# An adaLN attention block on one core: the first scale blocks move to ScalarE's queue, and the order of the k stage is redone

## The chip, the core and the metric

The kernel runs on one NeuronCore of a Trainium2 chip. The metric is the device time of one execution in microseconds (us). Thirteen runs of the kernel before gave a median of 98.5 us, from 97.48 to 99.33 us.

## What is computed

The reference is an attention layer with adaptive layer normalisation. With B = 2, N = 256, D = 1152 and all inputs in bf16:

```python
mod = (silu(c) @ w_mod).reshape(B, 6, 1, D)
shift_a, scale_a, gate_a = mod[:, 0], mod[:, 1], mod[:, 2]
h = layernorm(x) * (1 + scale_a) + shift_a
q, k, v = split(h @ wqkv)
p = softmax(q @ k.T * D ** -0.5)
return x + gate_a * (p @ v) @ wo
```

Three of the six parts of `w_mod` are used: shift, scale and gate. The host packs them, and the four other weights, so that each load is a block of whole rows for the 128 partitions.

## The kernel before

The 512 rows of x are four tiles of 128 tokens (t = 0 to 3; tiles 0 and 1 are batch 0, tiles 2 and 3 batch 1). D is nine slices of 128 (k = 0 to 8). The kernel first computes K transposed, one contraction slice k after the other, so that it can begin when the first rows of wK are there. This "k stage" is what the change touches. After it come Q (`wQ`), the scores, V (`wV`), the softmax, P·V and the output projection, all unchanged.

The parts of the k stage, by the names of their helpers:

- **Statistics.** Tiles 0 and 2 take their mean and variance on VectorE: three `stat_chunk` (bn_stats over 384 columns), then `stat_aggr`, then `stat_ln` and `stat_exp` on ScalarE give 1/std. Tiles 1 and 3 take them on ScalarE: `stat_sum` and `stat_sq` (two passes over 1152 columns), `stat_ln2`, `stat_exp`.
- **Normalise and transpose.** `norm(t, k0, k1)` on VectorE writes xn; `transposes(t, h)` on TensorE puts slices 0-1 (h = 0) or 2-8 (h = 1) into one of two PSUM buffers of the pool `psum_tp`; `evac_tp` copies them to xnT on ScalarE or VectorE.
- **Scale.** `silu_c` makes silu(c) and GpSimd repeats it into `scT_rep`. `scale_mods(gi, 0, 9)` multiplies it with one group of `wS` columns into the PSUM tile `psS` (which already holds ones); `copy_s1p(gi)` copies 1 + scale to SBUF. The groups are slices 0-1, 2-3, 4-5 and 6-8. `scaled_tp` takes the product straight from the transposes' PSUM tile; `scaled` (both tiles of a batch) and `scaled_t` (one tile) take it from xnT. All write hTs.
- **The products.** `k_step(k, n0, n1)` makes nine matmuls (one for each slice f of the output) over tokens n0 to n1 of batch 0. `k_step_b1(k, fs)` does the same for batch 1 and the listed f. Only f = 0 to 4 of batch 1 are accumulated in this pass; f = 5 to 8 follow later from the finished hTs.

The order is written out by hand. Each engine's instructions are recorded (`_Rec`, line 70, so that almost every instruction carries line 70 in the profile), and `pin` fixes that order (line 668). The long list of helper calls from line 307 to line 429 is therefore the order of TensorE, VectorE, ScalarE and SyncE at once: a call that stands earlier there stands earlier on its own engine.

Loads: x tiles, wK rows, scale groups and everything later go through SyncE's (SP) queue in the order of the list; only c goes through ScalarE's (ACT) queue (line 106). The order on SP is x0, x1, x2, scale group 0, wK0, x3, scale group 1, wK1, wK2, wK3, scale group 2, scale group 3, wK4 to wK8, then the shift, Q, gate, V and output weights. The framework gives each load one of eight completion semaphores in the order of its emission, and starts again with the first after the eighth. A load that takes a semaphore again waits on its issuing engine until the load that had it before has landed.

TensorE begins with dummy matmuls of ones (`junk(2)`, then the transpose of c and a matmul that fills psS with ones, then `junk(9)`), and only then comes to the transposes of x tile 0.

Of the kernel before, what the change touches and what calls it, by code (L numbers as in the profile page):

```python
# [15 lines left out]
def kernel(  # L16
# [14 lines left out]
    P = 128  # L31
    B, N, D = x.shape
# [68 lines left out]
    def load_x(eng, t):  # L101
        eng.dma_start(out=x_sb[:, t, :], in_=x_f[t * P : (t + 1) * P, :])

    nc.scalar.preload_act_table_set("natural_log_exp_and_others")
    load_x(syn, 0)
    sca.dma_start(out=c_sb, in_=c.rearrange("b (k p) -> (b k) p", p=P))

    wmpool = ctx.enter_context(tc.tile_pool(name="wmpool", bufs=1))
    wK = wpool.tile([P, KT, D], BF16)
# [11 lines left out]
        return rows  # L121

    wS_all = wmpool.tile([P, KT * D], BF16, tag="wS")
    S_GROUPS = SCALE_GROUPS
    wS = []
    for gi, (k0, k1) in enumerate(S_GROUPS):
        wS.append(wS_all[:, KT * P * k0 : KT * P * k1].rearrange("p (kk n) -> p kk n", kk=KT))
# [1 line left out]
    def load_scale(gi):  # L129
        k0, k1 = S_GROUPS[gi]  # L130
        cols = slice(KT * P * k0, KT * P * k1)
        src = w_scale[P * cols.start : P * cols.stop].rearrange("(p n) -> p n", p=P)
        syn.dma_start(out=wS_all[:, cols], in_=src)

    def load_wK(k):
        load_rows(wK[:, k : k + 1, :], wk[k])
# [37 lines left out]
    def stat_chunk(t, ch):  # L174
        vec.bn_stats(out=stats_t[t][:, ch, :], in_=x_sb[:, t, ch * CW : (ch + 1) * CW])

    def stat_aggr(t):
        vec.bn_aggr(out=mv_all[:, t, :], in_=stats_t[t])

    def stat_ln(t):  # L180
        sca.activation(out=lnv[:, t : t + 1], in_=mv_all[:, t, 1:2], func=ACT.Ln, bias=eps_t)

    def stat_exp(t):
        sca.activation(out=rstd[:, t : t + 1], in_=lnv[:, t : t + 1], func=ACT.Exp, scale=-0.5)
# [6 lines left out]
    def stat_sum(t):  # L191
        act_stats.add(t)
        sca.activation(out=scr, in_=x_sb[:, t, :], func=ACT.Copy, scale=-1.0 / D, accum_out=nmean[:, t : t + 1])

    def stat_sq(t):
        sca.activation(out=scr, in_=x_sb[:, t, :], func=ACT.Square, bias=nmean[:, t : t + 1],
                       accum_out=ssq[:, t : t + 1])

    def stat_ln2(t):
        sca.activation(out=lnv[:, t : t + 1], in_=ssq[:, t : t + 1], func=ACT.Ln, scale=1.0 / D, bias=eps_t)  # L200

    def norm(t, k0, k1):
        cs = slice(k0 * P, k1 * P)
        m_ap, m_op = (nmean[:, t : t + 1], ALU.add) if t in act_stats else (mv_all[:, t, 0:1], ALU.subtract)
        vec.tensor_scalar(
            out=xn[:, t, cs], in0=x_sb[:, t, cs], scalar1=m_ap,
            scalar2=rstd[:, t : t + 1], op0=m_op, op1=ALU.mult,
        )
# [5 lines left out]
    ten.matmul(psS.rearrange("p k r -> p (k r)"), lhsT=ones_w[0:1, 0:P],  # L214
               rhs=ones_w[0:1, 0 : KT * NR], start=True, stop=False, skip_group_check=True)
    sca.activation(out=e_sb, in_=cT_ps, func=ACT.Exp, scale=-1.0)
    sca.activation(out=e_sb, in_=e_sb, func=ACT.Ln, bias=1.0)
    sca.activation(out=e_sb, in_=e_sb, func=ACT.Exp, scale=-1.0)
    def silu_c():
        vec.tensor_tensor(  # L220
            out=scT_f.rearrange("p k b -> p b k"),
            in0=cT_ps.rearrange("p (b k) -> p b k", b=B),
            in1=e_sb.rearrange("p (b k) -> p b k", b=B),
            op=ALU.mult,
        )
        poo.tensor_copy(out=scT_rep, in_=scT_f.unsqueeze(2).to_broadcast([P, KT, NR // B, B]))
# [11 lines left out]
    def transposes(t, h):  # L238
        k0, k1 = ((0, KA), (KA, KT))[h]
        tp_t = psum_tp.tile([P, KT - KA, P], BF16, tag="tp")  # L240
        tps[t, h] = tp_t
        for k in range(k0, k1):
            ten.transpose(tp_t[:, k - k0, :], xn[:, t, k * P : (k + 1) * P], ident)

    def evac_tp(t, h, eng, c0, c1):
        base = h * KA
        copy = vec.tensor_copy if eng is vec else sca.copy
        copy(out=xnT[:, base + c0 : base + c1, t * P : (t + 1) * P], in_=tps[t, h][:, c0:c1, :])
# [7 lines left out]
    def scaled_tp(t, k, eng):  # L256
        b = t // NQ
        src = psS if t == 0 else s1p
        scale_by(eng, hTs[:, k, t * P : (t + 1) * P], tps[t, 0][:, k, :], src[:, k, b : b + 1])
# [10 lines left out]
    def scale_mods(gi, lo, hi):  # L270
        k0, k1 = S_GROUPS[gi]
        for kk in range(lo, hi):
            for j in range(k0, k1):
                ten.matmul(
                    psS[:, j, :], lhsT=wS[gi][:, kk, (j - k0) * P : (j - k0 + 1) * P], rhs=sc_rhs(kk),
                    start=False, stop=(kk == KT - 1), skip_group_check=True,
                )

    def copy_s1p(gi):
        k0, k1 = S_GROUPS[gi]  # L280
        vec.tensor_copy(out=s1p[:, k0:k1, :], in_=psS[:, k0:k1, 0:B])
# [24 lines left out]

    junk(9)
    stat_chunk(0, 2)
    stat_chunk(0, 1)
    stat_chunk(0, 0)  # L310
    silu_c()
    load_x(syn, 1)
    load_x(syn, 2)
    stat_aggr(0)
    stat_chunk(2, 2)
    stat_chunk(2, 0)
    stat_sum(1)
    stat_ln(0)
    stat_exp(0)
    norm(0, 0, 2)  # L320
    transposes(0, 0)
    stat_chunk(2, 1)
    norm(0, 2, KT)
    load_scale(0)
    stat_aggr(2)
    stat_sq(1)
    stat_ln2(1)
    scale_mods(0, 0, 9)
    stat_ln(2)
    scaled_tp(0, 0, vec)  # L330
    transposes(0, 1)
    scaled_tp(0, 1, vec)
    stat_exp(1)
    copy_s1p(0)
    stat_exp(2)
    evac_tp(0, 1, sca, 0, 7)
    load_wK(0)
    k_step(0, 0, P)
    norm(1, 0, 2)
    transposes(1, 0)  # L340
    norm(1, 2, KT)
    load_x(syn, 3)
    norm(2, 0, 2)
    scaled_tp(1, 0, vec)
    transposes(1, 1)
    k_step(0, P, N)
    scaled_tp(1, 1, vec)
    norm(2, 2, KT)
    transposes(2, 0)
    evac_tp(1, 1, vec, 0, 7)  # L350
    load_scale(1)
    scale_mods(1, 0, 9)
    copy_s1p(1)
    scaled(2, 0, vec)
    transposes(2, 1)
    load_wK(1)
    k_step(1, P, N)
    k_step(1, 0, P)
    scaled(3, 0, vec)
    evac_tp(2, 0, vec, 0, 2)  # L360
    stat_sum(3)
    stat_sq(3)
    load_wK(2)
    k_step(2, 0, N)
    stat_ln2(3)
    stat_exp(3)
    norm(3, 0, 2)
    evac_tp(2, 1, sca, 0, 7)
    transposes(3, 0)
    evac_tp(3, 0, sca, 0, 2)  # L370
    scaled_t(0, 3, sca)
    norm(3, 2, KT)
    transposes(3, 1)
    evac_tp(3, 1, vec, 0, 7)
    scaled_t(2, 3, sca)
    scaled_t(0, 2, vec)
    scaled_t(3, 3, vec)
    load_wK(3)
    k_step(3, 0, N)
    scaled_t(3, 2, sca)  # L380
    scaled_t(1, 3, sca)
    load_scale(2)
    scale_mods(2, 0, 9)
    alloc_b1()
    scaled_t(2, 2, vec)
    k_step_b1(0, [1, 2, 3, 4])
    k_step_b1(0, [0])
    k_step_b1(3, [1, 2, 3, 4])
    k_step_b1(2, [1, 2, 3, 4])
    copy_s1p(2)  # L390
    scaled_t(4, 3, vec)
    scaled_t(5, 3, vec)
    scaled_t(1, 2, vec)
    k_step_b1(1, [1, 2, 3, 4])
    scaled(4, 0, sca)
    scaled_t(5, 2, sca)
    scaled_t(4, 2, vec)
    load_scale(3)
    scale_mods(3, 0, 9)
    scaled(5, 0, vec)  # L400
    copy_s1p(3)
    scaled(6, 0, sca)
    scaled_t(6, 2, vec)
    scaled_t(6, 3, sca)
    scaled(7, 0, vec)
    scaled_t(7, 2, sca)
    scaled_t(7, 3, sca)
    scaled(8, 0, sca)
    scaled_t(8, 2, vec)
    scaled_t(8, 3, sca)  # L410
    load_wK(4)
# [4 lines left out]
    load_rest()  # L416
    k_step_b1(1, [0])
    k_step_b1(2, [0])
    k_step_b1(3, [0])
    k_step(4, 0, N)  # L420
    k_step_b1(4, [0])
# [246 lines left out]
    for rec in (ten, vec, sca, syn, poo):  # L668
        pin(rec.seq)

SCALE_GROUPS = ((0, 2), (2, 4), (4, 6), (6, 9))
_OUTS = [((2, 256, 1152), 'bfloat16')]

def _packed(inputs):

    import numpy as _np

    a = {n: _np.asarray(inputs[n]) for n in ('x', 'c', 'wqkv', 'wo', 'w_mod')}
    D = a['wo'].shape[0]
    P, KT, GK = 128, D // 128, 3  # L680

    def rows(w):
        return _np.ascontiguousarray(w).reshape(KT, P, D)

    def row_groups(w):
        w = rows(w).reshape(KT // GK, GK, P, D).transpose(0, 2, 1, 3)
        return _np.ascontiguousarray(w).reshape(KT // GK, P, GK * D)

    wqkv, w_mod = a['wqkv'], a['w_mod']
    scale = rows(w_mod[:, D : 2 * D]).transpose(1, 0, 2)  # L690
    scale = _np.concatenate([scale[:, :, k0 * P : k1 * P].reshape(-1) for k0, k1 in SCALE_GROUPS])
    return {
        'x': _np.ascontiguousarray(a['x']),
        'c': _np.ascontiguousarray(a['c']),
        'wk': rows(wqkv[:, D : 2 * D]),
        'wq': row_groups(wqkv[:, :D]),
        'wv': row_groups(wqkv[:, 2 * D :]),
        'w_scale': scale,
        'w_shift': row_groups(w_mod[:, :D]),
        'w_gate': row_groups(w_mod[:, 2 * D : 3 * D]),  # L700
        'wo': row_groups(a['wo']),
    }
# [21 lines left out]
```

## Time and profile before

| what | before |
|---|---|
| median of 13 runs | 98.5 us |
| the profiled execution's own time | 98.5 us |
| its span in the profile | 96.7 us |
| TensorE (PE) matmuls busy | 90.9 us, 94% |
| VectorE (DVE) busy | 63.0 us, 65% |
| ScalarE (ACT) busy | 33.9 us, 35% |
| DMA packets on SP's queue | 21.42 MB |
| DMA packets on ACT's queue | 0.05 MB |

The span leaves out 1.8 us that lie around the program. Times of instructions are counted from the start of the span. A line of the profile such as `8.18 0.64 PE ... psS<-scT_rep,wS_all ... x18` reads: from 8.18 us on, for 0.64 us, TensorE ran 18 matmuls that write psS from scT_rep and wS_all. A bracket at the end of such a line gives how long the engine was idle just before and what ended that idle time. PEld is the weight load that goes ahead of each matmul.

### The profile page before, as it was taken

Reading aid. Unit: us, or ns where it says so; the run is one execution under the profiler, and the core shown is the slowest. Engines: PE = TensorE matmul, PEld = TensorE weight load, DVE = VectorE, ACT = ScalarE, POOL = GpSimd, SP = SyncE. Lnnn points to the kernel's source line nnn. Section 1 sums busy time; section 2 is a strip of 40 time slices with the busy share of each in tenths; the row PEclk is TensorE's granted clock in tenths of the full one; section 3 lists DMA queues with packets and bytes.
Section 4 is the critical chain, followed back from the end, with each engine's and each line's share of the span. In section 5 each row is a group of like instructions: output and inputs, shape, how many; then the busy total and the mean of one; then the engine's idle time right before and its main releaser. Section 6 shows DMA issues by size and latency. Waiting matters only on the chain.

```text
span 96.7 us, 1888 instructions
## 1 busy us (share of the span) xinstructions
PE 90.9 (94%) x770; PEld 60.6 (63%) x770; DVE 63.0 (65%) x128; ACT 33.9 (35%) x78; POOL 15.6 (16%) x11
## 2 busy tenths in 40 slices
PE   4996999899999999999999999999999999999980
PEld 0235899788889744444448755666668766655570
DVE  2495957230270999999999939930008699998780
ACT  5495988180140910001952075332326400000010
POOL 2020000000000000000000000069999900020000
DMA  2979999999999999999993001131100000303132
GB/s 32 358 276 405 403 420 395 390 421 413 417 415 415 419 398 412 429 423 420 415 413 120 0 0 54 27 81 34 27 0 0 0 0 0 122 7 122 67 106 71
DMA packets 7379, 21.59 MB, mean 223 GB/s; under 512 B 2123, under 2 KB 2891, under 8 KB 7371
## 3 DMA queue, kind: packets, MB, share of 16 engines
q1 hardware_dynamic: 7200, 21.42, 57.5%
q8 instruction: 6, 0.10, 0.4%
q10 hardware_dynamic: 171, 0.05, 0.2%
q14 instruction: 2, 0.02, 0.0%
HBM read 19.76 MB, written 1.44 MB: 219 GB/s over the span
## 4 chain that ended last, share of the span: by engine, by line
PE 78%; DMA 17%; SPq 1%; ACT 0%; issue 0%
PE ps L70 67%; DMA wS_all<-in_w_scale_dram 17%; PE acc_t L70 8%; PE psH L70 2%; SPq L70 1%; PE psS L70 1%; ACT o_sb L70 0%
## 5 line engine op out<-in xcount | busy, mean ns | idle before, releaser
L70 POOL PARTITION_ALL_REDUCE gate_bc<-gacc x2 | 13.7, 6887 | 57.9 <-DVE gacc L70 57.9
L70 DVE SCALAR_TENSOR_TENSOR gacc<-wg_all,scT_f,gacc 128x1152 f32<-128x1152 bf16 x16 | 22.4, 1417 | 0.4
L70 PE MATMUL ps<-hT,wQ 128*128 128x512 bf16 x81 | 17.7, 379 | 0.0
L70 PE MATMUL ps<-wV,hT 128*128 128x384 bf16 x108 | 17.7, 326 | 0.0
L70 PE MATMUL ps<-rows_t,attnT 128*128 128x384 bf16 (+3 forms) x108 | 17.0, 319 | 0.0
L70 PEld LDWEIGHTS <-wK 128*128 128x128 bf16 x180 | 15.9, 98 | 1.6
L70 PEld LDWEIGHTS <-attnT 128*128 128x128 bf16 x117 | 11.2, 98 | 6.4
L70 PEld LDWEIGHTS <-hT 128*128 128x128 bf16 x108 | 10.6, 98 | 6.9
L70 PE MATMUL acc_t<-hTs,wK 128*128 128x256 bf16 (+1 forms) x144 | 14.8, 259 | 0.0
L70 PEld LDWEIGHTS <-wQ 128*128 128x128 bf16 x81 | 7.9, 98 | 9.4 <-issue 0.2
L70 ACT CAST v_sb<-ps 128x384 bf16<-128x384 f32 x12 | 5.8, 480 | 13.9 <-PE ps L70 13.9
L70 ACT CAST qkT<-ps 128x512 bf16<-128x512 f32 x11 | 5.6, 612 | 12.6 <-PE ps L70 12.6
L70 DVE CAST attnT<-ps 128x512 bf16<-128x512 f32 (+1 forms) x6 | 3.5, 603 | 9.5 <-PE ps L70 9.5
L70 DVE TENSOR_TENSOR ga<-ps,gate_bc 128x384 f32<-128x384 f32 (+3 forms) x12 | 6.5, 538 | 1.1 <-PE ps L70 1.0
L70 DVE TENSOR_TENSOR o_sb<-ga,x_sb 128x384 bf16<-128x384 f32 (+3 forms) x12 | 6.5, 541 | 0.4
L70 PE MATMUL acc_t<-ones_w 128*128 128x512 bf16 x11 | 5.0, 629 | 1.4 <-DVE ones_w L70 1.4
L70 ACT CAST o_sb<-ps 128x192 bf16<-128x192 f32 x1 | 0.3, 318 | 17.3 <-PE ps L70 17.3
L70 DVE CAST qkT<-acc_t 128x512 bf16<-128x512 f32 (+1 forms) x5 | 2.5, 578 | 5.8 <-PE acc_t L70 5.8
L70 ACT ACTIVATE hTs<-xnT,s1p 128x128 bf16<-128x128 bf16 (+1 forms) x12 | 4.3, 418 | 2.5 <-DVE s1p L70 2.2
L70 DVE BATCH_NORM_STATS2 st_t<-x_sb 128x6 f32<-128x384 bf16 x6 | 3.1, 551 | 2.3 <-DMA x_sb<-in_x_dram 2.3
L70 PE MATMUL ps<-hTs,wK 128*128 128x256 bf16 x36 | 4.3, 273 | 0.0
L70 PE MATMUL ps<-pT,v_sb 128*128 128x256 bf16 x36 | 4.1, 273 | 0.0
(59 smaller groups left out, 73.0 us busy)
## 6 DMA issues: line engine op xcount, KB each, us to landing
wK<-in_wk_dram SPq DMA_DIRECT2D x9, 288.0 KB, 9.5
rows_t<-in_w_shift_dram SPq DMA_DIRECT2D x3, 864.0 KB, 10.8
wQ<-in_wq_dram SPq DMA_DIRECT2D x3, 864.0 KB, 14.2
wg_all<-in_w_gate_dram SPq DMA_DIRECT2D x3, 864.0 KB, 14.1
wV<-in_wv_dram SPq DMA_DIRECT2D x3, 864.0 KB, 16.9
rows_t<-in_wo_dram SPq DMA_DIRECT2D x3, 864.0 KB, 16.9
wS_all<-in_w_scale_dram SPq DMA_DIRECT2D x3, 576.0 KB, 7.5
x_sb<-in_x_dram SPq DMA_DIRECT2D x4, 288.0 KB, 3.5
```

The lines of the kernel that those rows point to most:

```text
L70: r = fn(*a, **k)
```

## The change

c is loaded through SP, right behind x tile 0, and no longer through ACT. The columns of scale group 0 are loaded as two blocks, slice 0 and slice 1, of 288 KB each, through ACT's queue: the first behind the first of the three small activations that make silu(c), the second behind the last of them. The host packs these two slices apart. wK0 and wK1 now stand ahead of x tile 3 on SP, and wK2 ahead of scale group 2, wK3 ahead of scale group 3. `block_mods(0)` and `block_mods(1)` take the place of `scale_mods(0, 0, 9)`; the second half of tile 0's transposes follows them. VectorE normalises tile 0 after two of the three `stat_chunk` of tile 2 instead of around the third. The rest of the list is in a new order: among other things `k_step(1, 0, P)` moves up, `scaled(2, 0)` stays ahead of the transposes of tile 2, `evac_tp` of tile 2 swaps engines, `scale_mods(2)` moves ahead of `k_step(3)`, and `k_step_b1(2, [1, 2, 3, 4])` moves behind `scale_mods(3)`. No matmul is added or removed.

The core of the diff (the loads that a helper issues inside the list are those of the changed order above):

```diff
+    load_x(syn, 0)
+    syn.dma_start(out=c_sb, in_=c.rearrange("b (k p) -> (b k) p", p=P))
     nc.scalar.preload_act_table_set("natural_log_exp_and_others")
-    load_x(syn, 0)
-    sca.dma_start(out=c_sb, in_=c.rearrange("b (k p) -> (b k) p", p=P))
...
+    def load_block(j):
+        cols = slice(KT * P * j, KT * P * (j + 1))
+        sca.dma_start(out=wS_all[:, cols], in_=w_scale[P * cols.start : P * cols.stop].rearrange("(p n) -> p n", p=P))
...
     sca.activation(out=e_sb, in_=cT_ps, func=ACT.Exp, scale=-1.0)
+    load_block(0)
     sca.activation(out=e_sb, in_=e_sb, func=ACT.Ln, bias=1.0)
     sca.activation(out=e_sb, in_=e_sb, func=ACT.Exp, scale=-1.0)
+    load_block(1)
...
+    def block_mods(j):
+        w_j = wS_all[:, KT * P * j : KT * P * (j + 1)].rearrange("p (kk n) -> p kk n", kk=KT)
+        for kk in range(KT):
+            ten.matmul(
+                psS[:, j, :], lhsT=w_j[:, kk, :], rhs=sc_rhs(kk),
+                start=False, stop=(kk == KT - 1), skip_group_check=True,
+            )
...
     junk(9)
     stat_chunk(0, 2)
+    load_x(syn, 1)
+    stat_chunk(0, 0)
+    stat_sum(1)
     stat_chunk(0, 1)
-    stat_chunk(0, 0)
     silu_c()
-    load_x(syn, 1)
+    stat_aggr(0)
     load_x(syn, 2)
-    stat_aggr(0)
-    stat_chunk(2, 2)
-    stat_chunk(2, 0)
-    stat_sum(1)
+    stat_chunk(2, 1)
     stat_ln(0)
     stat_exp(0)
+    stat_chunk(2, 2)
+    stat_sq(1)
+    stat_ln2(1)
     norm(0, 0, 2)
     transposes(0, 0)
-    stat_chunk(2, 1)
+    block_mods(0)
+    block_mods(1)
     norm(0, 2, KT)
-    load_scale(0)
+    transposes(0, 1)
+    stat_chunk(2, 0)
+    scaled_tp(0, 0, vec)
     stat_aggr(2)
...
     load_wK(0)
     k_step(0, 0, P)
+    stat_exp(1)
     norm(1, 0, 2)
+    scaled_tp(0, 1, vec)
+    copy_s1p(0)
+    norm(1, 2, KT)
+    evac_tp(0, 1, sca, 0, 7)
     transposes(1, 0)
-    norm(1, 2, KT)
+    scaled_tp(1, 1, vec)
+    scaled_tp(1, 0, vec)
+    load_wK(1)
+    k_step(1, 0, P)
...
+    k_step(0, P, N)
     load_x(syn, 3)
...
-    k_step_b1(0, [1, 2, 3, 4])
-    k_step_b1(0, [0])
-    k_step_b1(3, [1, 2, 3, 4])
-    k_step_b1(2, [1, 2, 3, 4])
...
+    k_step_b1(0, [0])
+    scaled_t(3, 2, sca)
+    k_step_b1(0, [1, 2, 3, 4])
+    k_step_b1(1, [1, 2, 3, 4])
+    scaled_t(5, 2, sca)
+    scaled(4, 0, vec)
+    k_step_b1(3, [1, 2, 3, 4])
+    scaled_t(2, 2, vec)
     load_scale(3)
     scale_mods(3, 0, 9)
...
     k_step_b1(1, [0])
     k_step_b1(2, [0])
+    k_step_b1(2, [1, 2, 3, 4])
     k_step_b1(3, [0])
     k_step(4, 0, N)
```

More of the change, by code (lines that the diff above doesn't have):

```diff
@@ L123 @@
     wS_all = wmpool.tile([P, KT * D], BF16, tag="wS")
-    S_GROUPS = SCALE_GROUPS
+    S_GROUPS = ((0, 2), (2, 4), (4, 6), (6, 9))
     wS = []
@@ L308 @@
     stat_chunk(0, 2)
+    load_x(syn, 1)
+    stat_chunk(0, 0)
+    stat_sum(1)
     stat_chunk(0, 1)
-    stat_chunk(0, 0)
     silu_c()
-    load_x(syn, 1)
+    stat_aggr(0)
     load_x(syn, 2)
-    stat_aggr(0)
-    stat_chunk(2, 2)
-    stat_chunk(2, 0)
-    stat_sum(1)
+    stat_chunk(2, 1)
     stat_ln(0)
     stat_exp(0)
+    stat_chunk(2, 2)
+    stat_sq(1)
+    stat_ln2(1)
     norm(0, 0, 2)
     transposes(0, 0)
-    stat_chunk(2, 1)
+    block_mods(0)
+    block_mods(1)
     norm(0, 2, KT)
-    load_scale(0)
+    transposes(0, 1)
+    stat_chunk(2, 0)
+    scaled_tp(0, 0, vec)
     stat_aggr(2)
[L326 to L336, printed above, removed]
     load_wK(0)
     k_step(0, 0, P)
+    stat_exp(1)
     norm(1, 0, 2)
+    scaled_tp(0, 1, vec)
+    copy_s1p(0)
+    norm(1, 2, KT)
+    evac_tp(0, 1, sca, 0, 7)
     transposes(1, 0)
-    norm(1, 2, KT)
-    load_x(syn, 3)
[L343 to L347, printed above, removed]
+    scaled_tp(1, 1, vec)
+    scaled_tp(1, 0, vec)
+    load_wK(1)
+    k_step(1, 0, P)
+    stat_ln(2)
+    transposes(1, 1)
+    stat_exp(2)
+    norm(2, 0, 2)
+    k_step(0, P, N)
+    load_x(syn, 3)
+    stat_sum(3)
+    k_step(1, P, N)
     norm(2, 2, KT)
-    transposes(2, 0)
     evac_tp(1, 1, vec, 0, 7)
+    stat_sq(3)
+    stat_ln2(3)
     load_scale(1)
@@ L354 @@
     scaled(2, 0, vec)
+    transposes(2, 0)
     transposes(2, 1)
[L356 to L362, printed above, removed]
+    evac_tp(2, 1, vec, 0, 7)
+    stat_exp(3)
+    norm(3, 0, 2)
     load_wK(2)
     k_step(2, 0, N)
[L365 to L368, printed above, removed]
+    norm(3, 2, KT)
+    scaled(3, 0, vec)
+    evac_tp(2, 0, sca, 0, 2)
     transposes(3, 0)
+    load_scale(2)
+    scale_mods(2, 0, 9)
     evac_tp(3, 0, sca, 0, 2)
     scaled_t(0, 3, sca)
-    norm(3, 2, KT)
     transposes(3, 1)
     evac_tp(3, 1, vec, 0, 7)
-    scaled_t(2, 3, sca)
-    scaled_t(0, 2, vec)
-    scaled_t(3, 3, vec)
+    scaled_t(1, 2, vec)
     load_wK(3)
     k_step(3, 0, N)
-    scaled_t(3, 2, sca)
[L381 to L384, printed above, removed]
-    scaled_t(2, 2, vec)
-    k_step_b1(0, [1, 2, 3, 4])
-    k_step_b1(0, [0])
-    k_step_b1(3, [1, 2, 3, 4])
-    k_step_b1(2, [1, 2, 3, 4])
[L390 to L397, printed above, removed]
+    copy_s1p(2)
+    scaled_t(5, 3, vec)
+    scaled_t(3, 3, vec)
+    scaled(5, 0, vec)
+    scaled_t(1, 3, sca)
+    scaled_t(0, 2, sca)
+    alloc_b1()
+    k_step_b1(0, [0])
+    scaled_t(3, 2, sca)
+    k_step_b1(0, [1, 2, 3, 4])
[3 more added lines that the diff above has]
+    k_step_b1(3, [1, 2, 3, 4])
+    scaled_t(2, 2, vec)
     load_scale(3)
     scale_mods(3, 0, 9)
-    scaled(5, 0, vec)
+    scaled_t(4, 3, vec)
+    scaled_t(4, 2, sca)
+    scaled_t(2, 3, sca)
     copy_s1p(3)
@@ L403 @@
     scaled_t(6, 2, vec)
-    scaled_t(6, 3, sca)
+    scaled_t(6, 3, vec)
     scaled(7, 0, vec)
     scaled_t(7, 2, sca)
-    scaled_t(7, 3, sca)
-    scaled(8, 0, sca)
+    scaled_t(7, 3, vec)
+    scaled(8, 0, vec)
     scaled_t(8, 2, vec)
@@ L669 @@
         pin(rec.seq)
-SCALE_GROUPS = ((0, 2), (2, 4), (4, 6), (6, 9))
+SCALE_BLOCKS = ((0, 1), (1, 2), (2, 4), (4, 6), (6, 9))
 _OUTS = [((2, 256, 1152), 'bfloat16')]
@@ L690, in _packed @@
     scale = rows(w_mod[:, D : 2 * D]).transpose(1, 0, 2)
-    scale = _np.concatenate([scale[:, :, k0 * P : k1 * P].reshape(-1) for k0, k1 in SCALE_GROUPS])
+    scale = _np.concatenate([scale[:, :, k0 * P : k1 * P].reshape(-1) for k0, k1 in SCALE_BLOCKS])
     return {
```

## The prediction

> **What bounds the kernel now.** I read the chain of waits first.
>
> ```profile
> 8.15 10.19 DMA wS_all<-in_w_scale_dram
> 18.34 0.05 issue
> 18.39 0.87 PE psS L70 x27
> 19.26 7.97 PE acc_t L70 x73
> ```
>
> It shows that the end hangs on one load: scale group 3, issued at 8.15, lands at 18.34, and from then on TensorE alone carries the chain to 93.9. So only what shifts the start of that group's 27 matmuls, or the work left behind them, changes the time. How tight this wait is, the table by stretches tells (columns: stretch, length, then busy time and count of PE, PEld, DVE, ACT, POOL, clock, DMA share, GB/s):
>
> ```profile
> 7.00:8.18 1.18, 0.32 (x4) 0.14 (x2) 0.70 (x3) 1.05 (x6) 0.00 (x0) 1.00 1.03 387
> 8.18:18.08 9.90, 9.71 (x159) 8.79 (x159) 6.65 (x26) 7.34 (x16) 0.00 (x0) 1.00 1.03 405
> 18.08:18.39 0.31, 0.00 (x1) 0.00 (x1) 0.00 (x0) 0.00 (x0) 0.00 (x0) 1.00 1.08 401
> 18.39:60.00 41.61, 41.61 (x368) 28.12 (x369) 29.66 (x50) 14.05 (x35) 0.00 (x0) 1.00 0.82 334
> ```
>
> TensorE is busy 9.71 of 9.90 us from 8.18 to 18.08, then waits 0.31. The DMA engines are full all along at about 405 GB/s. So two limits lie 0.3 us apart: the row of TensorE work that starts at 8.18, and the bytes ahead of group 3. Then TensorE's timeline, for why it starts at 8.18:
>
> ```profile
> 2.64 0.19 PE L70 MATMUL cT_ps<-ident,c_sb 18*128 18x18 bf16 x1 [0.17 <-DMA c_sb<-in_c_dram]
> ...
> 3.19 4.02 PE L70 MATMUL acc_t<-ones_w 128*128 128x512 bf16 x9
> 7.01 0.32 PE L70 MATMUL tp_t<-ident,xn 128*128 128x128 bf16 x2
> 8.18 0.64 PE L70 MATMUL psS<-scT_rep,wS_all 128*128 128x56 bf16 x18 [0.86 <-DMA wS_all<-in_w_scale_dram]
> ```
>
> The dummy matmuls hold it until 7.01 (start of c's transpose to there: 4.37), and scale group 0 (landed 2.11 + 6.03 = 8.13) until 8.18. Last, ScalarE's timeline, because both new loads go into it:
>
> ```profile
> 2.87 0.19 ACT L70 ACTIVATE e_sb<-cT_ps 128x18 f32<-128x18 bf16 x1 [0.86 <-PE cT_ps L70]
> 3.08 0.47 ACT L70 ACTIVATE e_sb<-e_sb 128x18 f32<-128x18 f32 x2
> 4.40 1.16 ACT L70 ACTIVATE scr<-x_sb 128x1152 f32<-128x1152 bf16 x1 [0.84 <-DMA x_sb<-in_x_dram]
> ...
> 5.87 0.20 ACT L70 ACTIVATE rstd<-lnv 128x1 f32<-128x1 f32 x1
> ```
>
> The 1/std of tile 0 follows 1.47 us after the start of tile 1's sum.
>
> **What the Trainium skill says.** DMA: Bandwidth & Descriptors, section on the anatomy of one DMA: a DMA's semaphore wait is held by the issuing sequencer before dispatch. The trace agrees: SP issues group 3 at 8.15, right after group 0, whose semaphore it takes over, landed at 8.13. TensorE: Matmul & The Clock Gate, Part 1: ScalarE and VectorE are strict FIFO, so what stands behind such a wait stands still; no ACT wait of this kind is in the trace before. The DMA page again, "Issuing engines are not separate DMA queues": both queues share the same 16 engines and interleave, so the ACT queue brings no bandwidth, only a share ahead of SP's backlog; before, ACT carried 0.05 MB, so no run here shows it. The TensorE page, Part 1 too: the array's clock is halved until some microseconds of activity. The dummy matmuls' spacing, (7.01 - 3.19) / 9 = 0.424 us, against about 0.22 (17.7/81) at most later, agrees.
>
> **The change part by part.**
>
> *c behind x0 on SP.* Before, c was at TensorE at 2.63. Now it is issued when x0's issue is done (about 1.15 instead of 0.76) and queues behind x0, which landed at 0.72 + 2.94 = 3.66. Bounds: 3.0 (nothing but the later issue) and 3.8 (behind all of x0); I take 3.6. The dummies then end at 3.6 + 4.37 = 8.0 instead of 7.0, if all run at the half clock. Alone this is covered by the wait for the scale weights (up to 8.18), and only just.
>
> *Block 0.* The first activation runs 0.23 after c's transpose, at 3.85. The built program makes block 0's issue wait for the semaphore of x0 (3.66, already there), so it goes at about 4.05 and takes about 0.43 (SP's issue rows). silu(c) follows at about 5.1, as before (5.08), hidden. Landing: x0 took 2.94 from its issue; with half the engines' share for its 295 kB, 0.73 more. So 7.0 to 7.7; covered by the dummies.
>
> *Block 1: the added wait.* In the built program its issue waits for the semaphore of x2, although it needs nothing of x2. x2 landed at 1.64 + 3.74 = 5.38. Behind this wait on ScalarE stand tile 1's sum, the ln and exp for tile 0, and everything later; VectorE's norm of tile 0 waits for that exp, and TensorE's first transposes for the norm. So the sum starts at 5.38 + 0.43 = 5.8 instead of 4.40: +1.4 (bounds 0.8, if x2 lands earlier without the scale group behind it, and 1.8). The exp is then at 7.27, the norm 0.24 later (13.05 to 13.29 later in the trace) at 7.5, the transposes 0.40 later (9.32 to 9.72) at 7.9. That is level with the dummies' 8.0. The edit in VectorE's order (tile 0's norm ahead of one statistic) saves up to 0.46 of a bn_stats, but the norm now waits for ScalarE anyway: nothing. Block 1 itself, issued at 5.4, lands between 5.4 + 2.94 = 8.3 and 9.4, if block 0 is still ahead of it and the share is half; I take 8.9. The nine matmuls of block 1 wait for it, and all of TensorE's list behind them. They end at 8.9 + 9 x 0.027 ((8.66 - 8.18)/18) = 9.1, where before the group's ended at 8.66: +0.45.
>
> *The order behind.* From 8.66 to 18.08 the row took 9.42. `k_step_b1(2, [1, 2, 3, 4])` leaves it: 4 x 0.11 (8.13/73) = 0.44, so 8.98. The new list has its own waits. ScalarE runs tile 1's second pass, the evacuation of tile 0 and only then tile 3's statistics; these took 13.05 - 10.05 = 3.0 from sum to exp and now begin near 10.9, so tile 3's norm comes at 14.2 and its transposes at 14.6, with TensorE there at about 14.1 after k_step(2): 0.5. Tile 1's transposes wait for tile 1's exp (0.15), k_step(2) for scale group 1's copy and product (0.1). The row of before held about 0.5 of such waits (9.05 to 9.20, 9.85 to 10.20). Net +0.35 (bounds 0 and 0.9). TensorE reaches scale group 3 at 9.1 + 8.98 + 0.35 = 18.45.
>
> *Group 3's landing.* Ahead of it stand the same bytes as before: four x tiles, six scale slices, wK0 to wK3; merely their order differs. So again about 18.3. It needs 5.0 MB, which at 405 GB/s from 2.0 on is 14.4; the rest is a slow beginning and one lagging engine, as each of 6 instruction fetches holds an engine some 1.0 us (0.4% of 16 x 96.7 / 6). Bounds 17.0 and 19.0. TensorE at 18.45 is the later.
>
> *Behind group 3* stand now those four matmuls of step 2: +0.44, with all data long there. Loads of wK0 and wK1 ahead of x3: no k_step waited for wK before, so nothing gained; x3 lands about where it did, its first reader now comes later. From 19 on nothing differs; Q, gate and V weights keep their places on SP.
>
> Sum: 18.45 - 18.39 + 0.44 = +0.5 on the profiled execution, 98.5 (96.7 and 1.8 around), which equals the median: 99.0. A measurement of this kernel can tell about 0.5% (0.5 us) from no change.
>
> **Rivals.**
>
> *Absorbed.* TensorE arrives by 18.0 and group 3 lands by 18.0: +0.0 to +0.3, 98.7. For it: half the delay is only a block landing that I took in the middle of its bounds. Against: four matmuls' 0.44 must first be won back.
>
> *Not slower but faster, by group 3.* The one mechanism: the lagging engine's share. If the two blocks on the second ring spread the engines' work better and group 3 lands at 17.2, and block 1 by 8.3, TensorE comes at 8.55 + 8.98 = 17.5 and the end is 17.5 + 0.44 - 18.39 = -0.45, with warm dummies (clock up before 7) at most -0.8: 97.9. It decides from a landing of group 3 before 17.9. Against: the same bytes, the same fetches.
>
> *Late start in full.* x2 or block 1 late (9.8), and the half clock, [...] lasting into the first k_steps (9 matmuls at 0.107 by the TensorE page, an estimate, instead of 0.055: 0.5 each): +1.3 to +1.7, 100.0. For it: TensorE idles from 2.5 to 3.6 now.
>
> *The change doesn't reach what it names:* the head start of wK and of the norm is worth nothing, as priced above; this is part of all cases.
>
> **How the numbers follow.** Forecast (98.9 to 99.4) 0.39; absorbed 0.25; late start 0.22; faster 0.14. The forecast's case and the late start give slower by over 0.5% (0.58, with a little of the forecast inside the bound), absorbed and that rest 0.28, faster 0.14. Leaving out about 0.1 at each side: 98.2 to 100.2.
>
> **What would show it.** Right: ACT idle before tile 1's sum until about 5.8; the first transposes near 8.0; psS's first matmuls in two bursts of nine, the second at 8.5 to 9.3 after a wait for wS_all; a wait of some 0.5 before tile 3's transposes; no or little wait before group 3's matmuls, at about 18.4, and 77 instead of 73 matmuls in the stretch behind. Wrong: tile 1's sum at 4.4 to 5.0; group 3's 27 matmuls before 17.9.

## The result: 6.8% slower, and the profile after

The changed kernel takes 105.12 us in the median (104.15 to 105.80, 11 runs), the kernel before 98.83 us beside it (48 runs). The ratio is 1.068, 95% interval 1.064 to 1.072. The forecast was 99.0 us with a range from 98.2 to 100.2: the sign was right, the size was not. Medians are taken over all executions, while ratios compare only the undisturbed executions of both kernels, so that a median can lie further from the kernel before than its ratio says.

The profiled execution took 104.86 us with a span of 103.1 us, 6.4 more than before. The page's first parts show two things that were not there before, a poorly used array at the beginning and a clock that drops (40 slices of 2.58 us each, a digit is the share in tenths; PEclk is the clock that TensorE was granted):

```profile
PE   4591259999999999999999999999999999999980
...
PEclk9999556999999999999999999999999999999999
DMA  2899999999999999999920000112200000303032
```

TensorE is almost idle in the fourth and fifth slice (7.7 to 12.9), its clock is at half in the fifth and sixth and in part of the seventh, and the DMA engines are nevertheless full. So bytes move, but not those that TensorE waits for. TensorE's timeline says which:

```profile
4.30 3.47 PE L70 MATMUL acc_t<-ones_w 128*128 128x512 bf16 x9
8.74 0.29 PE L70 MATMUL tp_t<-ident,xn 128*128 128x128 bf16 x2 [0.96 <-DVE xn L70]
12.05 0.60 PE L70 MATMUL psS<-scT_rep,wS_all 128*128 128x56 bf16 x9 [3.03 <-DMA wS_all<-in_w_scale_dram]
14.05 0.60 PE L70 MATMUL psS<-scT_rep,wS_all 128*128 128x56 bf16 x9 [1.40 <-DMA wS_all<-in_w_scale_dram]
14.47 0.93 PE L70 MATMUL tp_t<-ident,xn 128*128 128x128 bf16 x7
15.19 1.17 PE L70 MATMUL acc_t<-hTs,wK 128*128 128x128 bf16 x9
```

Before, group 0's 18 matmuls ran at 8.18. Now block 0's nine run at 12.05 and block 1's at 14.05, each right after a wait for its load, 3.03 and 1.40 us. A k_step of nine matmuls takes 1.17 instead of 0.66. ScalarE's timeline shows when the two loads were issued:

```profile
3.97 0.19 ACT L70 ACTIVATE e_sb<-cT_ps 128x18 f32<-128x18 bf16 x1 [1.97 <-PE cT_ps L70]
3.98 0.38 ACTq L70 DMA_DIRECT2D wS_all<-in_w_scale_dram  x1
4.40 0.47 ACT L70 ACTIVATE e_sb<-e_sb 128x18 f32<-128x18 f32 x2 [0.24 <-ACT e_sb L70]
6.25 0.33 ACTq L70 DMA_DIRECT2D wS_all<-in_w_scale_dram  x1
6.63 1.16 ACT L70 ACTIVATE scr<-x_sb 128x1152 f32<-128x1152 bf16 x1 [1.75 <-DMA x_sb<-in_x_dram]
```

(A row with ACTq is the issue of a load.) Block 0 goes out at 3.98 and lands 8.0 us later, at 12.0; block 1 goes out at 6.25, when x tile 2 is there, and lands 7.8 later, at 14.0. The late issue of block 1 and ScalarE's wait were forecast. The landings were not. The DMA view of the stretch from 4.4 to 7.7, from the end of block 0's issue to the end of the dummies (a packet is one piece of a load; columns of the last line: queue, packets, MB, share of the 16 engines):

```profile
DMA packets 484, 1.01 MB, mean 307 GB/s; under 512 B 50, under 2 KB 50, under 8 KB 484
...
q1 hardware_dynamic: 484, 1.01, 94.0%
```

In these 3.3 us not one packet of ScalarE's queue (q10) moves; all 484 are of SP's (q1). Nor had one moved by 7.74, when SP's queue had moved 1.70 MB since the start of the span. From 8 to 12 it then has a good third:

```profile
q1 hardware_dynamic: 310, 0.96, 65.3%
q10 hardware_dynamic: 254, 0.53, 36.7%
```

The stretches show the rest (stretch, length, busy time and count of PE, PEld, DVE, ACT, POOL, clock, DMA share, GB/s):

```profile
8.74:14.47 5.73, 1.30 (x20) 0.98 (x21) 0.83 (x2) 1.30 (x4) 0.00 (x0) 0.65 1.02 395
10.50:17.30 6.80, 3.84 (x45) 3.70 (x46) 2.00 (x10) 1.83 (x4) 0.00 (x0) 0.50 1.03 408
14.47:24.28 9.81, 9.74 (x141) 9.24 (x139) 7.03 (x26) 7.19 (x18) 0.00 (x0) 0.85 1.03 408
```

In 5.73 us the array ran 20 matmuls. Then its row of work is as dense as before (9.74 of 9.81), at a mean clock of 0.85. The clock is at half from 10.5 to 17.3. Group 3 was there at 9.16 + 8.7 = 17.9 and its matmuls come only at 24.28: that load, the end of the chain before, holds nothing any more.

The chain that the profile prints for this execution goes over two loads of wK:

```profile
13.59 6.35 DMA wK<-in_wk_dram
19.95 1.13 PE acc_t L70 x9
...
24.44 0.70 PE psS L70 x27
25.14 8.41 PE acc_t L70 x77
```

Its first step is not to be believed. The nine matmuls at 19.95 are `k_step(2)`, and the load issued at 13.59 is wK7, which they don't read. TensorE was idle for 0.07 us there, and in three other runs below the same matmuls wait the same 0.07 us for VectorE's product. From 14.47 on TensorE has no gap above 0.1 us, so what made the row late are the two waits in front of it.

### The profile page after: what moved, and what is told of

Same layout as the page of the kernel before. It is cut to its first block, busy times and chain, and to the rows that moved or that the text cites. A ratio compares the mean times of both kernels' runs of the same rounds, so it can differ in the third digit from the quotient of the medians.

```text
span 103.1 us, 1886 instructions
## 1 busy us (share of the span) xinstructions
PE 92.0 (89%) x770; PEld 62.1 (60%) x770; DVE 63.8 (62%) x130; ACT 32.5 (32%) x76; POOL 15.6 (15%) x11
## 4 chain that ended last, share of the span: by engine, by line
PE 78%; DMA 15%; SPq 3%; issue 0%; ACT 0%
PE ps L70 63%; DMA wK<-in_wk_dram 15%; PE acc_t L70 12%; SPq L70 3%; PE psH L70 2%; PE psS L70 1%; PE tp_t L70 0%; ACT o_sb L70 0%
## 5 line engine op out<-in xcount | busy, mean ns | idle before, releaser
L70 PEld LDWEIGHTS <-wK 128*128 128x128 bf16 x180 | 16.9, 103 | 1.7 <-issue 0.2
L70 PE MATMUL acc_t<-hTs,wK 128*128 128x256 bf16 (+1 forms) x144 | 15.7, 271 | 0.1
L70 PEld LDWEIGHTS <-attnT 128*128 128x128 bf16 x117 | 11.2, 98 | 6.4
L70 PEld LDWEIGHTS <-hT 128*128 128x128 bf16 x108 | 10.6, 98 | 6.9
L70 ACT CAST qkT<-ps 128x512 bf16<-128x512 f32 x11 | 5.6, 612 | 12.6 <-PE ps L70 12.6
L70 PE MATMUL psS<-scT_rep,wS_all 128*128 128x56 bf16 x81 | 3.3, 196 | 4.4 <-DMA wS_all<-in_w_scale_dram 4.4
L70 PE MATMUL acc_t<-ones_w 128*128 128x512 bf16 x11 | 4.5, 572 | 1.4 <-DVE ones_w L70 1.4
L70 ACT CAST o_sb<-ps 128x192 bf16<-128x192 f32 x1 | 0.3, 318 | 17.3 <-PE ps L70 17.3
L70 PEld LDWEIGHTS <-wS_all 128*128 128x128 bf16 x81 | 2.9, 101 | 4.8 <-DMA wS_all<-in_w_scale_dram 4.7
L70 PE MATMUL tp_t<-ident,xn 128*128 128x128 bf16 x36 | 3.7, 242 | 1.0 <-DVE xn L70 1.0
```

The costliest lines, as they stand in the source:

```text
L70: r = fn(*a, **k)
```

## The experiments

Theory 1, formed from these lines: the blocks came late because a load's bytes are moved in the order of issue over both queues, and SP had issued x tiles 1 and 2, wK0, wK1, x tile 3 and (at 3.90, just ahead) group 1 before block 0. Rival theory 2: ScalarE's queue is starved as long as SP's has work; the third that it got from 8 to 12 speaks against this in its strict form. Rival theory 3: the wait of ScalarE, the list or c's place costs the time.

**The blocks on SP, behind x tile 2.**

```diff
     load_x(syn, 2)
+    load_block(0)
+    load_block(1)
...
-        sca.dma_start(out=wS_all[:, cols], ...)
+        syn.dma_start(out=wS_all[:, cols], ...)
```

The two calls between ScalarE's activations are gone here, and in every run below that puts the blocks elsewhere.

> The two blocks stay two loads but go through SP, right behind x tile 2 and ahead of wK0; all else is the changed kernel. Theory 1 (backlog): a load's bytes come in the order of issue over both queues, and in the changed kernel the blocks stood behind 1.5 MB that SP had issued first. Then block 0 lands at about 7.2 and block 1 at about 8.3 (group 0 as a whole landed at 8.13 before), the array does not idle, and the time is 98.8 to 99.8 us. Theory 2 (ScalarE's queue is starved while SP's has work): the same here. Theory 3 (the new list of steps, or c behind x0, costs the time): over 102 us.

Measured: 99.13 us, ratio 1.008 (1.004 to 1.012). The chain:

```profile
8.73 10.06 DMA wS_all<-in_w_scale_dram
18.79 0.05 issue
18.84 0.87 PE psS L70 x27
19.71 8.40 PE acc_t L70 x77
```

The load of group 3 bounds it again, as in the kernel before, and the 77 matmuls behind it (73 before) cost their 0.43 us (8.40 against 7.97). So nearly six of the 6.3 us lie in the place of the two loads. Of theory 3 the list and c's place fall: with wK's head start they cost 0.8% together. ScalarE's wait for x tile 2 is gone here too, and has a run of its own below. Theories 1 and 2 are both left.

**A short backlog on SP.** wK0, and with it all that SP issues behind it, waits for silu(c) (`SYNC` stands for the object that makes this dependency a wait).

```diff
-    load_wK(0)
+    first = load_wK(0)
+    tc.add_manual_dep(first.ins, silu[0].ins.name, SYNC, reason="late")
```

> The blocks stay on ScalarE's queue at the same place, but SP issues wK0 and everything behind it only after silu(c) (about 5.2), so that block 0, issued at about 4.0, has only x tiles 1 and 2 ahead of it; by the new numbering of semaphores block 1 no longer waits for x tile 2 and is issued near 4.8. Theory 1 (backlog): block 0 lands near 6.9 and block 1 near 7.8, time 98.5 to 100. Theory 2 (ScalarE's queue is starved while SP's has work, from 5.2 on it has): block 0 or at least block 1 still lands after 9.5, time over 101.

Measured: 99.95 us, ratio 1.016 (1.006 to 1.027). Block 0 landed 3.7 us after its issue, at 7.3, and block 1 at 8.06. From 5 to 7:

```profile
q10 hardware_dynamic: 252, 0.53, 86.5%
q1 hardware_dynamic: 11, 0.02, 5.6%
```

SP issued wK0 at 5.08, yet until 7 its queue moved 11 packets: now SP's load stands behind ScalarE's. (About 1.1 us of that pass without any queueing: block 0's own first packet moved 1.1 after its issue.) Theory 2 falls; theory 1 had both landings within 0.4. What is left, 1.6%, holds c's place behind x0, which is priced below, and the pause that this run forces on SP: TensorE waits 0.54 for wK and 0.46 for group 1's weights, and group 3 lands at 19.1.

**Half the backlog.** The same with x tile 3 as the load that waits, so that wK0 and wK1 stand ahead of the blocks.

```diff
-    load_x(syn, 3)
+    late = load_x(syn, 3)
+    tc.add_manual_dep(late.ins, silu[0].ins.name, SYNC, reason="late")
```

> As the run with the short backlog, but SP is held back only from x tile 3 on, so that wK0 and wK1 (0.59 MB, 1.45 us at 405 GB/s) stand ahead of the blocks. Theory 1 (backlog): the landings lie between: block 0 about 1.5 us later than with the short backlog, near 8.8, block 1 near 9.6, time 100 to 101.5. A theory in which a ready ScalarE queue takes turns with SP's from its issue on: block 0 under 8.0 and no difference in time to the short backlog (99.95).

Measured: 100.16 us, ratio 1.010 (1.007 to 1.014). Block 0 landed 4.9 after its issue, at 8.8, as theory 1 said, and block 1 at 10.6, a microsecond later than I expected. The ratio is not above the short backlog's, though theory 1 had expected a longer time and turn-taking none; what decides between them is the landing. SP's loads go out earlier here, and group 3 lands at 17.3 instead of 19.1, which may pay for the later blocks. This run also shows the order the other way round. SP issued x tile 3 at 5.24, after both blocks (3.95 and 4.63), and in the microsecond from 7.5 on its queue stands almost still:

```profile
q10 hardware_dynamic: 157, 0.32, 92.4%
q1 hardware_dynamic: 14, 0.02, 5.3%
```

**The blocks first on ScalarE's queue.**

```diff
+    load_block(0)
+    load_block(1)
     def load_wK(k):
```

> The blocks are the first instructions of ScalarE's queue, issued at 0.8 and 1.2, beside SP's x0, c and x1. Theory 1 (backlog): they land by 5.5, x tile 0 and c come up to 0.7 later and x tile 2 up to 1.5 later, and the time is 98.5 to 100. Theory 2 (ScalarE's queue is starved): they land after 8, as SP never runs dry, and x tile 0 is not later.

Measured: 99.53 us, ratio 1.010 (1.007 to 1.013). Block 0 landed at 4.9, block 1 at 5.7, and x tile 0, issued at the same moment on SP, at 4.7 instead of 3.6. Theory 2 falls once more. Now c, behind x0, comes late, and the row with it:

```profile
4.83 0.19 PE L70 MATMUL cT_ps<-ident,c_sb 18*128 18x18 bf16 x1 [2.35 <-DMA c_sb<-in_c_dram]
...
9.20 0.42 PE L70 MATMUL tp_t<-ident,xn 128*128 128x128 bf16 x2
9.41 1.05 PE L70 MATMUL psS<-scT_rep,wS_all 128*128 128x56 bf16 x18
```

**One load instead of two, in block 0's place.**

```diff
-    load_block(1)
...
-        cols = slice(KT * P * j, KT * P * (j + 1))
+        cols = slice(KT * P * j, KT * P * (j + 2))
```

> The two blocks become one load of 576 KB at block 0's place on ScalarE's queue (one packed block), so the second issue, and with it ScalarE's wait for x tile 2, is gone; SP's backlog stays. Theory 1 (backlog): the load starts near 7.7 like block 0 and lands between 12.5 and 14; time 103.5 to 105.5. Theory 3 (ScalarE standing still behind the wait for x tile 2 is what cost the time): tile 0's 1/std comes 2 us earlier, time below 101.

Measured: 103.33 us, ratio 1.048 (1.040 to 1.057). The whole group landed 8.3 us after its issue, at 12.2, a little before the bounds I gave. TensorE:

```profile
7.55 0.28 PE L70 MATMUL tp_t<-ident,xn 128*128 128x128 bf16 x2
12.21 1.02 PE L70 MATMUL psS<-scT_rep,wS_all 128*128 128x56 bf16 x18 [4.38 <-DMA wS_all<-in_w_scale_dram]
```

Without ScalarE's wait tile 0's transposes run at 7.55 instead of 8.74, and the array then waits 4.38 us for the load. So to be rid of that wait, which the prediction dwelt on, buys nothing by itself. What the wait does cost is the issue of block 1 at 6.25: with its bytes issued at 3.90 the last scale weights land 1.85 us earlier here, and the median falls by 1.8.

**The kernel before with only the two blocks on ScalarE's queue.**

```diff
     sca.activation(out=e_sb, in_=cT_ps, func=ACT.Exp, scale=-1.0)
+    load_block(0)
...
+    load_block(1)
...
-    load_scale(0)
...
-    scale_mods(0, 0, 9)
+    block_mods(0)
+    block_mods(1)
```

> The kernel before with its own list, its c load and its SP order, in which only scale group 0 goes as two blocks through ScalarE's queue, behind the same two activations as in the change. Theory 1 (backlog): SP has issued wK0, x3 and scale group 1 (1.2 MB) by then, block 0 lands at 10 to 11.5, block 1 at 11.5 to 13.5, time 102 to 105. If the new list or c behind x0 is what costs the time: under 100.

Measured: 103.63 us, ratio 1.052 (1.043 to 1.062). TensorE:

```profile
11.27 0.60 PE L70 MATMUL psS<-scT_rep,wS_all 128*128 128x56 bf16 x9 [1.94 <-DMA wS_all<-in_w_scale_dram]
12.83 0.60 PE L70 MATMUL psS<-scT_rep,wS_all 128*128 128x56 bf16 x9 [0.96 <-DMA wS_all<-in_w_scale_dram]
```

Block 0, issued at 4.41, landed 6.8 later, at 11.2; block 1 at 12.8. SP had by then issued wK1 and wK2 as well, 1.8 MB and not the 1.2 of the expectation. This one part alone makes most of the loss, with the old list and c in its old place.

**Dummies in the wait.**

```diff
+    junk(13)
     block_mods(0)
+    junk(7)
     block_mods(1)
```

> The changed kernel with 13 more dummy matmuls (128x512) ahead of block 0's matmuls and 7 ahead of block 1's, so that TensorE is not idle while it waits and keeps its clock; nothing else is changed. In the changed kernel the clock was at half from 10.5 to 17.3. If the half clock costs anything beside the waits, this gets back its share: nine matmuls of a k_step took 1.13 to 1.17 instead of 0.66 in 14 to 17.3, so about 1.0 us, to 104.1. If the waits alone set the time: 105.1, no change.

> The run with dummy matmuls in TensorE's wait once more, in more rounds, since its interval was wide. In the traces the stretch from block 1's last matmul to group 3's first took 9.97 us in the changed kernel (half clock from 10.5 to 17.3) and 8.84 with the dummies. If the half clock costs that 1.1 us also in the time: a ratio of 1.055 to 1.060 to the kernel before, against 1.068 of the changed kernel. If not: 1.065 or more.

Measured: 104.62 us, ratio 1.053 (1.039 to 1.066), and measured a second time 103.20 us, 1.047 (1.043 to 1.051), against 1.068 of the changed kernel. TensorE in the second run:

```profile
13.33 0.40 PE L70 MATMUL psS<-scT_rep,wS_all 128*128 128x56 bf16 x9
13.56 0.55 PE L70 MATMUL tp_t<-ident,xn 128*128 128x128 bf16 x7
14.11 0.66 PE L70 MATMUL acc_t<-hTs,wK 128*128 128x128 bf16 x9
...
22.39 0.86 PE L70 MATMUL psS<-scT_rep,wS_all 128*128 128x56 bf16 x27
```

A k_step takes 0.66 again, and the row from the end of block 1's matmuls to group 3 takes 22.39 - 13.56 = 8.83 instead of 24.28 - 14.47 = 9.81 (first matmul to first matmul in both timelines). So the half clock costs about 1.0 us of the 6.3; the second ratio says 2.1, more than I expected. In that profile block 1 was also there by 13.3 instead of 14.05, which may be the rest. The first of the two separates them: there block 1's matmuls began at 14.08, as late as in the changed kernel, the row took 8.84, and the profiled execution 103.74 us against 104.86. The earlier landing in the second goes with an earlier issue: block 0 went out at 3.66, ahead of group 1 (3.89) and long before the first added dummy (8.78). That fits theory 1, but no run was made to test it. The clock doesn't drop alike in every execution of the changed kernel: of its twelve executions (the profiled one is among them) seven had a mean clock of 0.965 to 0.967 and took 104.62 to 105.56 us, five of 0.998 or more; three of these took 104.15 to 104.28, two 105.67 and 105.80.

**c first, then the blocks, on ScalarE's queue.** The attempt at a better kernel that theory 1 points to.

```diff
-    syn.dma_start(out=c_sb, in_=c.rearrange("b (k p) -> (b k) p", p=P))
+    sca.dma_start(out=c_sb, in_=c.rearrange("b (k p) -> (b k) p", p=P))
...
+    load_block(0)
+    load_block(1)
     def load_wK(k):
```

> The changed list with c back as the first load of ScalarE's queue and the two blocks right behind it, at about 1.4 and 1.8, between SP's x tiles. Theory 1 (backlog): c comes near 2.7, so the dummies end near 7.0; block 0 lands by 5.5, block 1 by 6.5, x tile 2 by 7; the first scale matmuls start at 7.2 to 7.8 instead of 8.2. Time 97.3 to 98.6, at or below the kernel before, limited by group 3's landing (16.1 to 18.8 in the runs so far). If c behind x0 was harmless, no better than the 99.5 of the run with the blocks first.

Measured: 97.96 us, ratio 0.996 (0.993 to 0.999), a little faster than the kernel before. Its timeline:

```profile
7.36 0.28 PE L70 MATMUL tp_t<-ident,xn 128*128 128x128 bf16 x2 [0.66 <-DVE xn L70]
7.48 0.71 PE L70 MATMUL psS<-scT_rep,wS_all 128*128 128x56 bf16 x18
...
16.91 0.87 PE L70 MATMUL psS<-scT_rep,wS_all 128*128 128x56 bf16 x27
```

Block 0 landed at 5.3, before the transposes. Block 1 landed at 7.7, over a microsecond later than expected, but holds its matmuls for less than 0.1. Group 3's matmuls begin at 16.91 instead of 18.39.

**The same with step 2 back ahead of group 3.** 

```diff
     scaled_t(2, 2, vec)
+    scaled_t(2, 3, sca)
+    k_step_b1(2, [1, 2, 3, 4])
     load_scale(3)
...
-    scaled_t(2, 3, sca)
...
-    k_step_b1(2, [1, 2, 3, 4])
```

> As the run with c and then the blocks first on ScalarE's queue (97.96 us), with the four matmuls of step 2 for batch 1 put back ahead of group 3's matmuls. The prediction counted 0.44 us for their place. In that run TensorE came to group 3 about when it landed (16.86, matmuls at 16.91). If group 3's landing holds: up to 0.3 us faster, 97.6 to 97.8; if TensorE is the later of the two anyway: 97.9 to 98.0.

Measured: ratio 0.991 (0.987 to 0.996), from five executions; the median of all 22 is 99.94 us. The interval overlaps with that of the run before it; whether the four matmuls are worth their 0.44 us there is left open.

**The old list with the blocks right behind c.** The kernel before, where c already goes through ScalarE's queue.

```diff
+    load_block(0)
+    load_block(1)
     def load_wK(k):
...
-    load_scale(0)
...
-    scale_mods(0, 0, 9)
+    block_mods(0)
+    block_mods(1)
```

> The list of the kernel before with the two blocks right behind c on ScalarE's queue. This prices the new list: everything that the loads bring is the same as in the run with the changed list (97.96 us), only the order of steps is the old one. If the new list is needed for an early scale group: slower than that, 98.3 to 98.8. If only the landing of the blocks matters: 97.8 to 98.1.

Measured: ratio 0.999 (0.996 to 1.003), median 99.74 us. Against 0.996 with the new list: the intervals overlap. So the list is worth 0.3% as measured, which is not clear of noise. In its profile group 3's matmuls start at 18.13, after waits of the old list such as 0.38 for ScalarE's evacuation of tile 0, 1.2 us later than with the new list.

**c's place alone.** The first run (blocks on SP behind x tile 2), with c on ScalarE's queue.

```diff
-    syn.dma_start(out=c_sb, in_=c.rearrange("b (k p) -> (b k) p", p=P))
+    sca.dma_start(out=c_sb, in_=c.rearrange("b (k p) -> (b k) p", p=P))
```

> As the run with the blocks on SP right behind x tile 2 (99.13 us), but c goes through ScalarE's queue again as in the kernel before. This prices c's place: c comes near 2.65 instead of 3.5 and the dummies end near 7.0 instead of 7.9. If the dummies' end is what starts TensorE's row there: scale matmuls up to 0.9 us earlier, 98.3 to 98.7. If group 3's landing (18.8 in that run) holds the end anyway, as the chain of that run says: no change, 99.1.

Measured: 98.36 us, ratio 0.995 (0.993 to 0.998), against 1.008 with c behind x0. So c's move to SP costs 1.3%, and the whole loss of the first run is c's. In this profile group 3 landed at 17.4, before TensorE came (17.92), so its landing didn't hide c's gain: where that load lands differs by up to 3 us between the profiles of these kernels (16.1 to 19.1).

## Why the prediction was wrong, step by step

- **What bounds the kernel: right for before.** The chain ended on group 3's load, and that of the first experiment ends on it again (18.79). In the changed kernel the load bounds nothing. That the first experiment's 99.13 us lie beside the forecast is luck: the forecast had late blocks in it.
- **c behind x0: right.** Forecast at 3.6, first used at 3.75. "Covered, and only just" was too kind: once the blocks are in time, it costs 1.3%.
- **Block 0's issue: right** (4.05, measured 3.98). **Its landing: wrong, and this is the step that failed.** The prediction said "x0 took 2.94 from its issue; with half the engines' share for its 295 kB, 0.73 more. So 7.0 to 7.7". It landed at 12.0. The premise in front of it, that the ACT queue brings "only a share ahead of SP's backlog", read a turn-taking from the moment of issue into "both queues share the same 16 engines and interleave". The sharing is as the page says: q10 did get a third from 8 to 12. But the turns began only at 7.74, when 1.70 of the 2.4 MB that SP had issued before the block had gone. So the order is that of issue in the main and not to the last packet: group 1, issued 0.08 us ahead of block 0, landed at 12.6, after it. With about 0, 0.6 and 1.5 MB issued by SP after x tile 2 and before the block, it landed 3.7, 4.9 and 8.0 us after its issue. 1.5 MB at 405 GB/s are 3.6 us, an amount the prediction had all numbers for; with the 3.7 of the run without them they make 7.3. The old list fits less well: 1.8 MB make 8.1, measured 6.8. Nearly all these loads have one size, so the runs don't tell whether bytes or the number of loads ahead count.
- **Block 1: the wait right, its worth wrong.** Its issue waited for x tile 2 (6.25 against 5.4 forecast, as x tile 2 landed at 2.00 + 4.2 = 6.2), so that tile 1's sum began at 6.63, beyond the 6.2 of its bounds. Landing forecast 8.9, at most 9.4, measured 14.0, from the same failed premise. ScalarE's standstill, priced in detail, is hidden by the longer wait for the load.
- **The order behind: about right in its sum, for the wrong reason.** Forecast 8.98 + 0.35 = 9.33 from block 1's last matmul to group 3, measured 9.81, with the clock at half in the first third, which the prediction had only as a rival at the very start. At full clock it took 8.83: the forecast wait of 0.5 before tile 3's transposes did not come. In that run ScalarE's statistics of tile 3 ran from 15.39 to 18.57, as long after block 1 as forecast, but TensorE was not waiting there: `k_step(2)` ran from 17.85 for 1.14, and the transposes started right behind it, at 19.01.
- **Group 3's landing: right** (about 18.3 forecast, 17.9 measured) and irrelevant. **The four matmuls of step 2: right**, 8.41 against 7.97 in the chain, 0.44.
- **The rivals.** "Late start in full" named the right mechanism, a late block and the half clock, with bounds that came from the same premise: +1.3 to +1.7 for what was +6.3. Of the two signs of being wrong neither came: tile 1's sum was not early and group 3's matmuls not before 17.9. A second burst far beyond 9.3 was not among them.

The sum with the measured term: block 1's matmuls end at 14.47 instead of 8.66 (+5.8), the row behind takes 9.81 instead of 9.42 (+0.4), the wait of 0.31 for group 3 is gone, four matmuls come behind it (+0.44): +6.3, measured +6.4 in the span.

## What to carry to other kernels

In these runs a load on another engine's queue was not ahead of what a busy queue had issued already. To estimate its landing, add up the bytes issued before it on both queues and not yet moved, divide by the rate, and only then add the load's own time; with the bytes behind x tile 2 and the 3.7 us of the run without them, this met the three measured landings within 1.3 us. What is needed first has to be issued first, before the backlog, and small things (c here, 1.3%) ahead of large ones. The waits of 3.03 and 1.40 us on TensorE were paid for once more, by about 1.0 us, since the matmuls after them ran at half the clock for a while; after the waits of 0.36 and 1.36 in the run with half the backlog a k_step took 0.66 as at full clock.

## What the runs showed that I had not expected

- Two hardware queues behaved in the main like one queue by order of issue: 0 packets of the second in 3.3 us with the first one's backlog, and 14 of the first beside 157 of the second in 1 us, with the first one's load issued after the second's and over 2 us old. Why they keep this order no run shows.
- The clock was at half in the changed kernel from about 10.5 to 17.3, after the array had run two matmuls between 8 and 12; it came back only some 3 us after work was dense again. The Trainium skill, TensorE: Matmul & The Clock Gate, Part 1, says that an idle window of about 3.4 us brings this on and a busy one ends it. The trace agrees in the end of it (14.05 to 17.3) and in the length, 6.8, two such windows. It doesn't in the beginning: at 10.5 the array had been empty for only 1.5 us, since 9.03, and the 3.4 us up to then hold the last dummies and two matmuls. Dummy matmuls in the wait kept the clock at 1.0.
- The semaphore that a load happens to get can tie it to a load that it has nothing to do with. Here block 1 went out at 6.25, though the activation ahead of it was done by 4.9; one load in place of two, without that wait, brought 1.8 us in the median.
